# mLSTM cell with a squared-ReLU FFN: rounding of the weights shared between engines, sigmoid gates, the first decay rows through TensorE, and the first FFN group in two halves

## The chip, the cores and the metric

The kernel runs on one core of a Trainium2 chip. The time is device microseconds of one execution, as the median of several runs. One more execution is recorded by the hardware profiler; its times of single instructions are what the text argues from. The engines are TensorE (PE; its weight loads are listed as PEld), VectorE (DVE), ScalarE (ACT), GpSimd (POOL) and SyncE (SP), whose queue issues most transfers.

## The reference

```python
# q, k, v, o_gate: (4, 8, 768, 40); i_gate, f_gate: (4, 8, 768); float32
for t in range(S):
    m_new = np.maximum(f_gate[:, :, t] + m, i_gate[:, :, t])
    f_stab = np.exp(f_gate[:, :, t] + m - m_new)
    i_stab = np.exp(i_gate[:, :, t] - m_new)
    m = m_new
    C = f_stab[:, :, None, None] * C + i_stab[:, :, None, None] * np.einsum('bhd,bhe->bhde', vt, kt)
    n = f_stab[:, :, None] * n + i_stab[:, :, None] * kt
    h_tilde = np.einsum('bhde,bhe->bhd', C, qt)
    nq = np.einsum('bhd,bhd->bh', n, qt)[:, :, None]
    o = 1.0 / (1.0 + np.exp(-o_gate[:, :, t]))
    y[:, :, t] = o * h_tilde / np.maximum(np.abs(nq), 1.0)
...
x = y.transpose(0, 2, 1, 3).reshape(3072, 320)
h = np.maximum(x @ w_in, 0.0)          # w_in: (320, 2048), float64
return (h * h @ w_out).astype(np.float32)   # w_out: (2048, 320), float64
```

## The kernel before, in words

The recurrence runs in 24 chunks of 128 tokens (six for each of the four sequences); the FFN takes four chunks at a time as a group of 512 tokens, six groups in all. Everything is float32. The order of the work on every engine is the order in which the program is written: each engine works through its own list, and SyncE issues its transfers in program order, so that one that must wait holds back those behind it.

At the start `do_gates` (L206) turns the gates into A, the sum of the logarithms of the decays in a chunk, with two scans on VectorE; A goes to DRAM (L215) and comes back as `A_bc`, one row for all partitions (`load_A`, L243). A chunk then has five steps:

- `weigh` (L251): GpSimd adds A_bc and the input's exponent (L255), cuts off the future (L259), ScalarE takes exp (L265): W. Then the output gate 1/(1+exp(-o)): VectorE, ScalarE, VectorE, VectorE (L268 to L271). GpSimd scales the values (L274).
- `transposes` (L278): TensorE turns k and q, ScalarE copies kT and VectorE qT (L287).
- `scores` (L289): sixteen short matmuls, two heads of a pair side by side (L296), then VectorE multiplies by W to P (L301).
- `attend` (L305): the state's share (hi, L312), the state's update (dC, L319), the chunk's own share (hp, L326), then VectorE and GpSimd put them together (L332 to L358); x is the row that the FFN takes.
- `turn_rows` (L360): TensorE turns x, ScalarE copies it into xT (L368).

The weights come as float64, as pairs of 32-bit words. `Rounding` brings them in pieces of 128 rows by 512 (w_in, ten pieces) or by 320 columns (w_out, sixteen), three ahead, and rounds each to float32: six VectorE instructions (L172 to L188) build the truncated value and the remainder, GpSimd adds the two (L191), VectorE puts the sign on (L158), one step later. The first group's four chunks are worked off alone, with two rounding steps beside each; then w_out's pieces are rounded beside the eight parts of the first group's first FFN matmul.

That matmul is `ffn1` (L372): a part makes two slices of d_ff for 512 tokens, four matmuls of 128 rows (L382) and two of 64 rows side by side (L387), then ScalarE's relu (L390) and VectorE's square (L391). The second is `ffn2` (L393, L398): two halves for each chunk. From the ninth part of group 0 on, each chunk of the recurrence is spread over four parts of the FFN.

Of the kernel before, what the change touches and what calls it, by code (L numbers as in the profile page):

```python
# [9 lines left out]
F32 = mybir.dt.float32  # L10
# [6 lines left out]
P = 128  # L17
# [6 lines left out]
# exp of anything below -104 is 0 in float32  # L24
# [4 lines left out]
def kernel(  # L29
# [36 lines left out]
    GT = 4                   # chunks in an FFN group  # L66
    NG = NT // GT
    W = GT * P
    KR = DM - 2 * P          # rows of the last slice of d_model
# [3 lines left out]
    ld = ctx.enter_context(tc.tile_pool(name="ld", bufs=4))  # L73
    prep = ctx.enter_context(tc.tile_pool(name="prep", bufs=3))
# [6 lines left out]
    first = ExitStack()      # what only the start needs; the FFN's tiles lie there later  # L81
    gates = first.enter_context(tc.tile_pool(name="gates", bufs=1))
    conv_in = first.enter_context(tc.tile_pool(name="conv_in", bufs=2))
# [9 lines left out]
    keep = gates.tile([BH, NB, P], F32)  # L93

# [4 lines left out]
    def make_consts():  # L99
# [7 lines left out]
        # 1 where the row's head of the pair is the column's  # L107
# [9 lines left out]
    in_pieces = []  # L117
    for f0 in range(0, DFF, 512):
        for a in range(2):
            in_pieces.append((w_in[:, a, f0 : f0 + 512], [(slice(0, P), win_w[a * P : (a + 1) * P, f0 : f0 + 512, :])]))  # L120
# [383 lines left out]
```

## Time and profile before

| | us |
|---|---|
| median of 3 runs | 705.58 |
| lowest and highest | 704.78, 705.85 |
| span of the profiled execution | 704.2 |
| TensorE busy in it | 600.5 |
| VectorE busy | 343.4 |
| GpSimd busy | 152.6 |
| ScalarE busy | 123.2 |

The execution's time has been given with its span alone; the median of the runs lies 1.4 us above this span. Busy times are sums over the whole span and mix stages, so windows and the chain of waits have to say which engine bounds which stage. A row of the timeline has the start, the duration, engine, line, operation, what is written and read, and in brackets how long the engine had been idle and who ended that. A row of the groups has the busy time, the mean in nanoseconds of one instruction, and the idle time ahead of them. A mean contains what instructions were held up while they ran.

### The profile page before, as it was taken

The page shows a single profiled execution, that of the slowest core. Times are in us where ns is not written, and L with a number is a line of the kernel's source. Part 1 is how long each engine was busy: PE and PEld are TensorE (multiplying, and loading weights), DVE is VectorE, ACT ScalarE, POOL GpSimd, SP SyncE. Part 2 cuts the span into 40 slices and gives each one's busy share as a digit, 9 for nine tenths or more (in the row PEclk, how much of TensorE's full clock was granted, in tenths as well). Part 3 has the DMA queues.
Part 4 walks back from the last instruction along what each step waited for, and adds up shares of the span by engine and source line. Part 5 has one row for each costly group of instructions (what it writes and reads, how often), then busy time and mean ns, then how long its engine had stood idle before and what let it go on. Part 6 is the DMA issues. An engine that isn't in the chain of part 4 may idle for free.

```text
span 704.2 us, 7122 instructions
## 1 busy us (share of the span) xinstructions
PE 600.5 (85%) x2708; PEld 384.3 (55%) x2708; DVE 343.4 (49%) x621; ACT 123.2 (17%) x242; POOL 152.6 (22%) x159
## 2 busy tenths in 40 slices
PE   1236566919469999999999999999999999999998
PEld 1136554414147754477644777554776457763475
DVE  6588895978873335542344523354334434302200
ACT  1201100111011113210231211133111321102200
POOL 1444432322322320321122123202230222000000
PEclk9999856968769999999999999999999999999999
DMA  9976673432514331332132224221330000000000
GB/s 158 233 156 123 123 111 81 76 86 76 107 35 86 76 47 31 67 69 56 48 68 39 56 60 78 47 56 43 76 76 22 0 1 1 19 20 0 1 19 19
DMA packets 141297, 44.79 MB, mean 64 GB/s; under 512 B 109424, under 2 KB 138096, under 8 KB 141264
## 3 DMA queue, kind: packets, MB, share of 16 engines
q1 hardware_dynamic: 141264, 44.35, 31.5%
q8 instruction: 21, 0.34, 0.2%
q14 instruction: 12, 0.10, 0.1%
HBM read 40.30 MB, written 4.03 MB: 63 GB/s over the span
## 4 chain that ended last, share of the span: by engine, by line
PE 68%; DVE 21%; POOL 3%; issue 2%; ACT 2%; SPq 2%; DMA 1%; POOLq 0%; ACTq 0%; DVEq 0%
PE o_ps L398 30%; PE h_ps L382 18%; PE h_ps L387 5%; PE hp L326 4%; DVE og L271 4%; PE sc L296 4%; DVE g L391 3%; PE hi L312 2%; DVE mag L172 2%; PE dC L319 2%; DVE top L182 2%; DVE rem L188 2%; PE tp L283 2%; SPq L241 1%; DVE mag L173 1%
## 5 line engine op out<-in xcount | busy, mean ns | idle before, releaser
L398 PE MATMUL o_ps<-w_out,g 128*128 128x320 f32 x768 | 216.0, 438 | 0.0
L382 PE MATMUL h_ps<-xT,w_in 128*128 128x512 f32 x384 | 179.6, 611 | 0.0
L398 PEld LDWEIGHTS o_ps<-w_out,g 128*128 128x128 f32 x768 | 144.8, 192 | 58.9 <-issue 2.6
L391 DVE TENSOR_TENSOR g<-r_sb 128x512 f32<-128x512 f32 x96 | 63.6, 704 | 135.0 <-ACT r_sb L390 135.0
L382 PEld LDWEIGHTS h_ps<-xT,w_in 128*128 128x128 f32 x384 | 70.5, 193 | 85.3 <-issue 80.1
L296 PE MATMUL sc<-qT,kT 40*128 40x128 f32 x384 | 35.9, 329 | 70.8 <-DVE qT L287 44.6
L390 ACT ACTIVATE r_sb<-h_ps 128x512 f32<-128x512 f32 x96 | 52.2, 595 | 211.9 <-PE h_ps L387 211.9
L296 PEld LDWEIGHTS sc<-qT,kT 40*128 40x128 f32 x384 | 30.6, 227 | 84.0 <-issue 57.2
L191 POOL TENSOR_TENSOR rem<-rem,top 128x320 f32<-128x320 f32 (+1 forms) x26 | 32.1, 1236 | 110.8 <-DVE rem L188 110.8
L387 PE MATMUL h_ps<-xT,w_in 64*128 64x512 f32 x192 | 54.2, 641 | 0.0
L301 DVE TENSOR_TENSOR P_sb<-sc,W_sb 128x512 f32<-128x512 f32 x48 | 30.8, 684 | 45.3 <-PE sc L296 45.3
L326 PE MATMUL hp<-va,P_sb 128*128 128x41 f32 x384 | 51.7, 299 | 0.7 <-ACT xT L368 0.7
L271 DVE RECIPROCAL og<-og 128x320 f32<-128x320 f32 x24 | 51.7, 2153 | 0.8
L326 PEld LDWEIGHTS hp<-va,P_sb 128*128 128x128 f32 x384 | 50.5, 212 | 0.9 <-ACT xT L368 0.9
L255 POOL TENSOR_TENSOR W_sb<-A_bc,b_T 128x1024 f32<-128x1024 f32 x24 | 45.7, 1905 | 14.7 <-DMA A_bc<-a_rows 14.5
L345 POOL TENSOR_TENSOR C_sb<-C_sb,Cd 128x328 f32<-128x328 f32 x16 | 14.1, 884 | 152.7 <-DVE C_sb L337 152.4
L270 DVE TENSOR_SCALAR og<-og 128x320 f32<-128x320 f32 x24 | 12.4, 518 | 69.1 <-ACT og L269 69.1
L404 ACT COPY y_sb<-o_ps 128x320 f32<-128x320 f32 x24 | 10.2, 426 | 204.7 <-PE o_ps L398 204.7
L265 ACT ACTIVATE W_sb<-W_sb 128x1024 f32<-128x1024 f32 x24 | 25.4, 1057 | 60.0 <-POOL W_sb L259 60.0
L358 POOL COPY x_sb<-x_sb 128x64 f32<-128x64 f32 x24 | 6.9, 289 | 126.6 <-DVE x_sb L357 126.6
L387 PEld LDWEIGHTS h_ps<-xT,w_in 64*128 64x128 f32 x192 | 14.4, 184 | 36.4 <-issue 36.4
L319 PE MATMUL dC<-vw,kq 128*128 128x82 f32 x160 | 23.8, 297 | 10.1 <-DVE P_sb L301 10.1
(63 smaller groups left out, 445.9 us busy)
## 6 DMA issues: line engine op xcount, KB each, us to landing
A_bc<-a_rows SPq DMA_DIRECT2D x24, 512.0 KB, 4.4
raw<-in_moe_w_out_dram SPq DMA_DIRECT2D x16, 320.0 KB, 2.9
kq<-in_k_dram SPq DMA_DIRECT2D x26, 160.0 KB, 3.3
kq<-in_q_dram SPq DMA_DIRECT2D x26, 160.0 KB, 4.3
va<-in_v_dram SPq DMA_DIRECT2D x26, 160.0 KB, 3.8
o_sb<-in_o_gate_dram SPq DMA_DIRECT2D x26, 160.0 KB, 3.8
raw<-in_moe_w_in_dram SPq DMA_DIRECT2D x8, 512.0 KB, 4.1
out_dram<-y_sb SPq DMA_DIRECT2D x24, 160.0 KB, 1.8
```

Source lines behind the costliest of these rows:

```text
L191: nc.gpsimd.tensor_tensor(rem[:], rem[:], top[:].bitcast(F32), op=ALU.add)
L255: nc.gpsimd.tensor_tensor(d["W"][:], d["A"][:], b_T[:, b, c, :].unsqueeze(2).to_broadcast([P, H, P]), op=ALU.add,)
L271: nc.vector.reciprocal(d["og"][:], d["og"][:])
L296: nc.tensor.matmul(sc[i][:, j, :], lhsT=d["kT"][rows, j, :], rhs=d["qT"][rows, j, :], start=True, stop=True,)
L301: nc.vector.tensor_tensor(d["P"][:, i], sc[i][:], d["W"][:].rearrange("p (j two) t -> p j two t", two=2)[:, :, i, :], op=ALU.mult,)
L319: nc.tensor.matmul(dC[:, j].rearrange("p h d -> p (h d)"), lhsT=d["kq"][:, 0, 2 * j : 2 * j + 2, :].rearrange("p h d -> p (h d)"), rhs=d[" ...
L326: nc.tensor.matmul(hp[:, h, :], lhsT=d["P"][:, h % 2, h // 2, :], rhs=d["va"][:, h, :], start=True, stop=True,)
L382: nc.tensor.matmul(h[:], lhsT=w_in[:, a, fb * P : (fb + 1) * P], rhs=xT[:, a, :], start=(a == 0), stop=False,)
L387: nc.tensor.matmul(hs[i][:], lhsT=w_in2[rows, p, :], rhs=xT[rows, 2, :], start=False, stop=True)
L390: nc.scalar.activation(r[:], hs[i][:], AF.Relu)
L391: nc.vector.tensor_tensor(st["g2"][:, 2 * p + i, :], r[:], r[:], op=ALU.mult)
L398: nc.tensor.matmul(o_ps[:], lhsT=st["g2"][:, fb, j * P : (j + 1) * P], rhs=w_out[:, fb, :], start=(fb == 0), stop=(fb == NF - 1),)
```

## The change

- The rounding is spread out: ScalarE takes the absolute value of the high word, read as a float, and turns the low word into a float just above 2, whose last bits carry the rounding (two ACTIVATEs); VectorE bounds the high word, shifts it by three bits, and puts the sign in with an exclusive or; GpSimd adds the two words as 32-bit integers, which gives the rounded weight. The buffers of raw words are four, those of the two intermediate tiles two each; w_in and w_out are one list of pieces, ordered as the first FFN matmul takes them.
- The output gate is one ACTIVATE with Sigmoid, in place, for runs of 2, 2, 4, 8 and 8 chunks; the gates have loads of their own.
- For chunks 0 and 1 A does not come through DRAM: TensorE spreads it over the partitions with a matmul against a selector (`weigh_near`), in two halves of four heads.
- The gates' input i and the store of A are issued by ScalarE; one subtraction of the gate stage is GpSimd's; the buffers of A_bc and of W are two where they were three.
- The first group's first FFN matmul runs in two halves of 256 tokens (`ffn1_half`), each of four quarters with four slices of d_ff; the first half starts when two chunks are through, with the rounding of w_in beside it and that of w_out beside the second half.

The core of the diff:

```diff
+        nc.gpsimd.memset(sel[:], 0.0)
+        nc.gpsimd.affine_select(
+            sel[:], sel[:], compare_op=ALU.not_equal, fill=1.0, base=0, pattern=[[-1, H], [0, P]], channel_multiplier=1,
+        )
...
+        def words(self):
...
+            nc.scalar.activation(mag[:, :w], raw[:, :, 1].bitcast(F32), AF.Abs)
+            low = conv.tile([P, 512], F32, name="low")
+            nc.scalar.activation(low[:, :w], raw[:, :, 0].bitcast(U32), AF.Copy, bias=2.0, scale=2.0 ** -51)
+            self.a.append((mag, low))
+
+        def join(self):
...
+            nc.vector.tensor_scalar(
+                mag, mag, scalar1=word_as_float(0x38000000), scalar2=word_as_float(0x47EFFFFF),
+                op0=ALU.max, op1=ALU.min,
+            )
+            nc.vector.tensor_scalar(bits, bits, scalar1=3, scalar2=None, op0=ALU.logical_shift_left)
+            nc.vector.scalar_tensor_tensor(
+                bits, in0=self.raws[n][:, :w, 1], scalar=-0x80000000, in1=bits,
+                op0=ALU.bitwise_and, op1=ALU.bitwise_xor,
+            )
+            nc.gpsimd.tensor_tensor(dst.bitcast(I32), bits, low.bitcast(I32), op=ALU.add)
+            self.b.append(None)
+            self.fetch()
...
         def step(self):
...
+            if len(self.b) < len(pieces):
+                if len(self.a) == len(self.b):
+                    self.words()
+                self.words()
+                self.join()
...
     def do_gates():
         nc.vector.tensor_tensor_scan(m_sb[:], f_sb[:], i_sb[:], -1e30, op0=ALU.add, op1=ALU.max)
+        nc.gpsimd.tensor_tensor(i_sb[:], i_sb[:], m_sb[:], op=ALU.subtract)
...
-        nc.sync.dma_start(A_d[:, :], A_sb[:])
-        nc.vector.tensor_tensor(i_sb[:], i_sb[:], m_sb[:], op=ALU.subtract)
+        nc.scalar.dma_start(A_d[:, :], A_sb[:])
...
+    def sigmoid(s):
+        nc.scalar.activation(st[s]["og"], st[s]["og"], AF.Sigmoid)
...
+    def weigh_near(s):
...
+        for i in range(2):
+            hh = slice(i * H2, (i + 1) * H2)
+            A = ps_h.tile([P, H2, P], F32, name="A_ps", tag="h_ps")
+            for h in range(H2):
+                nc.tensor.matmul(
+                    A[:, h, :], lhsT=sel[:, i * H2 + h, :],
+                    rhs=A_sb[:, c * P : (c + 1) * P], start=True, stop=True,
+                )
+            Wh = d["W"][:, hh, :]
+            nc.vector.tensor_tensor(Wh, A[:], b_T[:, b, c, hh].unsqueeze(2).to_broadcast([P, H2, P]), op=ALU.add)
+            nc.scalar.activation(d["dec"][:, hh], A[:, :, P - 1], AF.Exp)
+            nc.gpsimd.affine_select(
+                Wh, Wh, compare_op=ALU.is_ge, fill=-1e30, base=0, pattern=[[0, H2], [1, P]], channel_multiplier=-1,
+            )
+            nc.scalar.activation(Wh, Wh, AF.Exp)
...
-        d["og"] = prep.tile([P, H, D], F32, name="og")
-        nc.vector.tensor_scalar_max(d["og"][:], d["o"][:], -88.0)
-        nc.scalar.activation(d["og"][:], d["og"][:], AF.Exp, scale=-1.0)
-        nc.vector.tensor_scalar_add(d["og"][:], d["og"][:], 1.0)
-        nc.vector.reciprocal(d["og"][:], d["og"][:])
...
+    def ffn1_half(g, half, pp):
...
+        for i in range(2):
+            for n in range(2):
+                fb = 4 * pp + 2 * n + i
+                for a in range(2):
+                    nc.tensor.matmul(
+                        hs[i][:, n, :], lhsT=w_in[:, a, fb * P : (fb + 1) * P], rhs=xT[:, a, cols],
+                        start=(n == 0 and a == 0), stop=False,
+                    )
...
+    for half in range(2):
+        for u in range(4):
+            s = 2 * (half + 1) + u // 2
+            if u % 2 == 0:
+                score(s)
+                turn_rows(s - 1)
+            else:
+                if u == 1:
+                    for r in range(s, s + 2 + 2 * half):
+                        sigmoid(r)
+                attend_on(s)
+            for _ in range(IN_DONE[u] - rounding.done if half == 0 else 4):
+                rounding.step()
+            ffn1_half(0, half, u)
+            if u % 2 == 0:
+                weigh_on(s + 1)
+            else:
+                transposes(s + 1)
+            if half == 0:
+                load_o(4 + u)
+    assert rounding.done == len(pieces)
+    turn_rows(5)
...
-    for n in range(NU * NG):
+    for n in range(NPAIR, NU * NG):
```

`IN_DONE` is (3, 5, 8, 10): so many pieces are rounded before quarters 0 to 3 of the first half. Where things stand on the engines is shown at three places. On VectorE, beside the first group's first FFN matmul, the order of before has this for one piece of w_out (`raw` are the words, `rem` the remainder, `g` the squared rows):

```order
L172 TENSOR_SCALAR mag<-raw 128x320
L173 TENSOR_SCALAR mag<-mag 128x320
L179 TENSOR_SCALAR top<-mag 128x320
L182 SCALAR_TENSOR_TENSOR top<-mag,top 128x320
L186 TENSOR_SCALAR mag<-top 128x320
L188 SCALAR_TENSOR_TENSOR rem<-raw,mag 128x320
L158 SCALAR_TENSOR_TENSOR w_out<-raw,rem 128x320
L391 TENSOR_TENSOR g_723<-r_sb 128x512 x2
```

Two such pieces stand in a part, and the squares of a part behind them. In the changed kernel the last piece of a quarter of the second half, and what follows it, reads:

```order
L183 TENSOR_SCALAR mag<-mag 128x320
L187 TENSOR_SCALAR mag<-mag 128x320
L188 SCALAR_TENSOR_TENSOR mag<-raw,mag 128x320
L475 TENSOR_TENSOR g_448<-r_sb 128x2x256 x2
L335 COPY qT<-tp 128x512
L354 TENSOR_TENSOR P_sb<-sc,W_sb 128x512 x2
```

Three instructions a piece are left, four pieces stand in a quarter, and the squares, the copy of qT and P stand behind all four. On GpSimd, at the same place, the order of before (`Cd` and `C_sb` are the state, `W_sb` the weighing of a chunk to come):

```order
L191 TENSOR_TENSOR rem<-rem,top 128x320 x2
L340 TENSOR_TENSOR Cd<-C_sb,dec 128x328
L345 TENSOR_TENSOR C_sb<-C_sb,Cd 128x328
L358 COPY x_sb<-x_sb 128x64
L191 TENSOR_TENSOR rem<-rem,top 128x320 x4
L255 TENSOR_TENSOR W_sb<-A_bc,b_T 128x1024
L259 AFFINE_SELECT W_sb<-W_sb 128x1024
```

and of the changed kernel:

```order
L192 TENSOR_TENSOR w_out<-mag,low 128x320 x4
L304 TENSOR_TENSOR W_sb<-A_bc,b_T 128x1024
L308 AFFINE_SELECT W_sb<-W_sb 128x1024
L393 TENSOR_TENSOR Cd<-C_sb,dec 128x328
L398 TENSOR_TENSOR C_sb<-C_sb,Cd 128x328
L411 COPY x_sb<-x_sb 128x64
L192 TENSOR_TENSOR w_out<-mag,low 128x320 x8
```

The add now writes the weight itself, and each add stands directly behind one VectorE instruction of its piece and ahead of the weighing and the state. On TensorE, before, the first FFN matmul of group 0 stands behind all four chunks of the group (`tp` are transposes, `sc` scores, `h_ps` the first FFN matmul):

```order
L367 MATMUL tp<-ident,x_sb 128x128 x3
L296 MATMUL sc<-qT,kT 128x128 x8
L382 MATMUL h_ps<-xT,w_in 128x512 x4
L387 MATMUL h_ps<-xT,w_in_99 128x512 x2
L312 MATMUL hi<-C_sb,qT 128x82 x4
```

and in the changed kernel behind the second chunk's rows:

```order
L420 MATMUL tp<-ident,x_sb 128x128 x3
L331 MATMUL tp<-ident,kq_89 128x128 x8
L344 MATMUL sc<-qT,kT 128x128 x8
L420 MATMUL tp<-ident,x_sb 128x128 x3
L459 MATMUL h_ps<-xT,w_in 128x256 x8
L466 MATMUL h_ps<-xT,w_in_100 128x256 x4
L365 MATMUL hi<-C_sb,qT 128x82 x4
```

The half matmuls have 256 columns instead of 512, twice as many of them, and chunk 2's attend comes behind the first quarter.

More of the change, by code (lines that the diff above doesn't have):

```diff
@@ L446 @@
-    assert rounding.n == len(in_pieces) and not rounding.last
+    for _ in range(3):
+        rounding.fetch()
+    load(1)
+    load_o(0)
+    load_o(1)
+    rounding.fetch()
+    transposes(0)
+    do_gates()
+    rounding.words()
+    weigh_near(0)
+    values(0)
+    transposes(1)
+    scores(0)
+    rounding.step()
+    weigh_near(1)
+    values(1)
     first.close()
     ffn = ctx.enter_context(tc.tile_pool(name="ffn", bufs=2))
-    conv_out = ctx.enter_context(tc.tile_pool(name="conv_out", bufs=2))
@@ L458 @@
         if at == 0:
-            do(scores, s)
+            do(score, s)
         if at == 1:
```

211 lines of the change are left out of this document (120 added, 91 removed).

## The prediction

> **What bounds the kernel now.** I read the page first, then a table of time windows, then the chain of waits around the place where the first FFN group hands over to its second matmul, and then the list of who waited for whom in the first 200 us. The page gives the span, and two rows of 40 slices of 17.6 us each: the busy tenths of VectorE (DVE) and the TensorE clock that was granted, in tenths.
>
> ```profile
> span 704.2 us, 7122 instructions
> DVE  6588895978873335542344523354334434302200
> PEclk9999856968769999999999999999999999999999
> ```
>
> VectorE is at 5 to 9 tenths for the first eleven slices (about 195 us) and at half of that or less afterwards; the clock dips only there. Two windows say the same of TensorE (PE, then weight loads, VectorE, ScalarE, GpSimd, clock):
>
> ```profile
> 180.00:200.00 20.00, 3.12 (x9) 0.87 (x7) 15.05 (x27) 3.25 (x6) 7.41 (x7) 0.66 0.31 92
> 300.00:400.00 100.00, 99.60 (x472) 63.33 (x471) 40.92 (x73) 20.24 (x40) 18.29 (x19) 1.00 0.27 55
> ```
>
> From 300 to 400 us TensorE is busy 99.6 of 100 us: nothing but its own work bounds that stage. From 180 to 200 us it is busy 3.1 of 20 us, and VectorE 15. The chain and the waits name the border between the two stages and who is late ahead of it:
>
> ```profile
> 200.31 2.08 PE sc L296 x16
> 202.39 6.74 PE o_ps L398 x16
> ...
> POOL rem L191 <- DVE rem L188: 101.9, 24, 12.9
> PE sc L296 <- DVE qT L287: 26.0, 2, 16.2
> ```
>
> At 200.31 us the scores of chunk 6 start, then the second FFN matmul of group 0. Ahead of that GpSimd waits 102 us for VectorE's rounding, and TensorE waits for VectorE's copies. So the kernel is a start of 200.3 us bound by VectorE and a tail of 704.2 - 200.3 = 503.9 us bound by TensorE. The changed kernel enters its last loop at the same place (chunk 6's scores, then group 0's second matmul) and runs the same TensorE work from there. I keep the tail at 503.9 us and work out only when chunk 6's scores start. The 1.4 us between this span and the median of 705.58 us are added at the end. Runs spread over 1.1 us, so 0.2% (1.4 us) is what can be told from no change.
>
> **The change, part by part.** *Rounding.* Seven VectorE instructions per piece become three (a max/min, a shift, a combination), two go to ScalarE, and GpSimd's add now makes the result. The nearest rows are those of the same form, 512 and 320 wide:
>
> ```profile
> L173 DVE TENSOR_SCALAR mag<-mag 128x512 f32<-128x512 f32 x10 | 5.2, 521 | 0.3
> L179 DVE TENSOR_SCALAR top<-mag 128x512 int32<-128x512 int32 x10 | 4.3, 427 | 0.3
> L182 DVE SCALAR_TENSOR_TENSOR top<-mag,top 128x512 int32<-128x512 int32 x10 | 6.9, 692 | 0.3
> L173 DVE TENSOR_SCALAR mag<-mag 128x320 f32<-128x320 f32 x16 | 5.8, 361 | 0.6
> L179 DVE TENSOR_SCALAR top<-mag 128x320 int32<-128x320 int32 x16 | 5.2, 327 | 0.5
> L182 DVE SCALAR_TENSOR_TENSOR top<-mag,top 128x320 int32<-128x320 int32 x16 | 7.9, 492 | 0.6
> ```
>
> On VectorE alone a piece costs 0.52 + 0.43 + 0.69 = 1.64 us (512) or 0.36 + 0.33 + 0.49 = 1.18 us (320). But the add of a piece runs beside the VectorE work of the next, and the timeline shows what that does:
>
> ```profile
> 34.40 1.38 POOL L191 TENSOR_TENSOR rem<-rem,top 128x512 f32<-128x512 f32 x1 [7.68 <-DVE rem L188]
> 34.69 1.37 DVE L173 TENSOR_SCALAR mag<-mag 128x512 f32<-128x512 f32 x1
> ...
> 125.76 0.32 DVE L172 TENSOR_SCALAR mag<-raw 128x320 int32<-128x320 int32 x1
> 125.92 0.87 POOL L191 TENSOR_TENSOR rem<-rem,top 128x320 f32<-128x320 f32 x1 [12.94 <-DVE rem L188]
> 126.11 0.87 DVE L173 TENSOR_SCALAR mag<-mag 128x320 f32<-128x320 f32 x1
> ...
> 139.56 1.04 POOL L191 TENSOR_TENSOR rem<-rem,top 128x320 f32<-128x320 f32 x1 [2.40 <-DVE rem L188]
> 139.80 1.35 DVE L391 TENSOR_TENSOR g<-r_sb 128x512 f32<-128x512 f32 x1
> ```
>
> One scalar instruction slips in ahead of the add (125.76); the next (126.11) takes 0.87 us for 0.33 and ends 0.19 us behind the add. So in the change a piece's max/min slips in, its shift waits for the add of the piece before: 0.08 us to the add, 0.87, 0.19, then 0.49 for the combination make 1.63 us per 320 piece. For 512, from the pair at 34.4: 0.08 + 1.38 + 0.28 + 0.69 = 2.45 us. The integer add itself stands in no row; I take the float add's 0.87 and 1.38, which moves the same bytes, with half (only a gain of some 6 us, since VectorE's own work then shows) and twice as bounds.
>
> The last pair shows that the square (two operands out of SBUF) is held as well, 1.35 us for 0.70. The Trainium skill differs here: Advanced Engine Details and Errata, VectorE Performance Modes, names only two-port instructions as blocked by GpSimd. By that the squares and the gate products behind an add would run through, and the sum would be some 3 us less; the row at 139.80 speaks against it.
>
> ScalarE's two reads of a piece run one piece ahead, beside VectorE; at the relu's 0.60 us per 512 (below) twice that is under the 2.45 us per piece, and at double price it would come level.
>
> *Weighing, gates and the first rows.* The first two chunks' decay rows come over TensorE instead of a round trip through DRAM; the gates' reciprocal leaves VectorE (a gain in the tail that TensorE's 99.6% hides). The rows that I use:
>
> ```profile
> 10.48 0.94 DVE L217 TENSOR_TENSOR i_sb<-i_sb,A_sb 32x768 f32<-32x768 f32 x1
> 12.20 0.82 PE L221 MATMUL tp<-ident,A_sb 32*128 32x32 f32 x6
> 41.55 3.55 PE L326 MATMUL hp<-va,P_sb 128*128 128x41 f32 x16
> 115.45 5.01 PE L382 MATMUL h_ps<-xT,w_in 128*128 128x512 f32 x8
> 121.45 1.12 PE L312 MATMUL hi<-C_sb,qT 128*128 128x82 f32 x8
> 125.04 3.68 PE L382 MATMUL h_ps<-xT,w_in 128*128 128x512 f32 x8
> 128.65 1.13 PE L387 MATMUL h_ps<-xT,w_in 64*128 64x512 f32 x4
> ...
> 129.08 0.49 DVE L332 TENSOR_TENSOR num<-hi,eA_T 128x328 f32<-128x328 f32 x1
> 131.94 0.49 DVE L357 TENSOR_TENSOR x_sb<-x_sb,dm 128x320 f32<-128x320 f32 x1
> ...
> L391 DVE TENSOR_TENSOR g<-r_sb 128x512 f32<-128x512 f32 x96 | 63.6, 704 | 135.0 <-ACT r_sb L390 135.0
> L390 ACT ACTIVATE r_sb<-h_ps 128x512 f32<-128x512 f32 x96 | 52.2, 595 | 211.9 <-PE h_ps L387 211.9
> L255 POOL TENSOR_TENSOR W_sb<-A_bc,b_T 128x1024 f32<-128x1024 f32 x24 | 45.7, 1905 | 14.7 <-DMA A_bc<-a_rows 14.5
> L301 DVE TENSOR_TENSOR P_sb<-sc,W_sb 128x512 f32<-128x512 f32 x48 | 30.8, 684 | 45.3 <-PE sc L296 45.3
> L259 POOL TENSOR_SCALAR_AFFINE_SELECT W_sb<-W_sb 128x1024 f32<-128x1024 f32 x24 | 26.2, 1092 | 1.8
> L265 ACT ACTIVATE W_sb<-W_sb 128x1024 f32<-128x1024 f32 x24 | 25.4, 1057 | 60.0 <-POOL W_sb L259 60.0
> L287 DVE COPY qT<-tp 128x512 f32<-128x512 f32 x24 | 15.9, 662 | 5.8 <-PE tp L283 5.8
> L227 ACT ACT_TABLE_LOAD x1 | 1.3, 1283 | 0.7 <-PEq L488 0.7
> ```
>
> *Stage A, to the second chunk's output.* Gate work ends at 11.42 us now; one subtraction moves to GpSimd: 10.5. Twelve small transposes (11.42 to 13.02): 12.1. TensorE then runs cold: eight decay matmuls twice (unseen; four pairs of scores take 2.08, so 0.52 each one by one, 4.2, bounds 2.1 and 4.2), transposes, two scores and the state product at 2.1 each as for scores, and 3.55 for the output: 12.1 + 8.4 + 8.4 + 3.55 = 32.4, and 1.3 of waits for a copy (0.6) and a first product (0.7): 33.7. VectorE: the rest of the output about 2.0, a piece 1.64, P 2 x 0.68: 38.7. The second output on TensorE 3.55, its VectorE tail 2.5 (129.08 to 132.43 is 3.35 for all, 0.8 of it early): 44.8.
>
> *Stage B, to the first half of FFN matmuls.* Chunk 2's weights on GpSimd (behind the second output's copy in its queue) and ScalarE 1.9 + 1.1 + 1.06, a piece on ScalarE 1.2, a copy 0.6, scores 2.1, three transposes and a copy 1.4: 9.3. The first half starts at 54.1 us.
>
> *Stage C, first half.* A half part has as many columns as a part now: 125.04 to 128.65 and 1.13 make 4.7, and 1.33 more when it starts cold (5.01 against 3.68): four times 6.0 is 24.1. Two chunks' attends: TensorE 3.6 (121.45 to 125.04) and VectorE's tail 2.55, 12.3 in all. Three times the FFN waits for a pair of pieces: 1.64 + 2.45 + 1.46 = 5.55, 16.7 in all. Two turns to the next scores: two relus 1.2, a square 0.7, a copy 0.66, scores 2.1: 9.3. One P: 1.4. Sum 63.7, so 117.8 us.
>
> *Stage D, second half.* Here VectorE is the bound. Per quarter four pieces, 1.18 + 3 x 1.63 = 6.1, and two squares of which the second waits for the last add, 1.5: 7.6. A chunk has two quarters, P 1.4, a copy 0.66, an attend 3.35, 1.0 for instructions held by the weighing (1.9 and 1.1 on GpSimd right behind the adds), and 2.1 for scores: 23.7. Two chunks less one scores: 45.3. Chunk 6's scores start at 163.1 us against 200.3.
>
> *Tables.* Exp and sigmoid now alternate: six more table loads ahead of that point, at 1.28 each. One could lie on the path, ahead of chunk 2's product with its gate: relu's end, exp 1.06 and 0.2, load 1.28 and a sigmoid of about 0.5 take 3.1 us, while TensorE's 3.6 and VectorE's first steps run beside them: hidden. The Trainium skill, ScalarE: Activation LUTs, What ACT_TABLE_LOAD costs, puts a switch at 2.66 us with its drain. By that, an estimate from that page, the gate would come level or some 0.8 us late, and the sum be that much more; this trace has one load and cannot show a drain.
>
> *Sum.* 163.1 + 503.9 = 667.0 us of span, with 1.4 around it: 668 us.
>
> **The rivals.** *Faster: TensorE warm and VectorE less held.* If adds held VectorE only as far as its own work (1.28 and 1.74 us per piece with gaps), 16 x 0.35 + 1.8 + 2.0 go, four warm starts save 5.3, and a warm stage A about 5: some 20 us, 649 us. For it: after 8 us of dense work the clock was full (121.45). Against: the start stays broken by waits. 0.20.
>
> *A queue.* SyncE's list is in program order, and a load that must wait for TensorE stands ahead of later pieces and decay rows.
>
> ```profile
> SPq L241 <- PE dC L319: 18.6, 2, 15.4
> ```
>
> One load blocked it for 15.4 us now. In the change chunk 4's loads (released by chunk 0's output, 33.7) stand ahead of pieces, chunk 3 and its decay rows, which are due at about 50. If these come 12 us late: 680 us. 0.15.
>
> *Slower: the integer add.* It makes every weight and stands between VectorE's steps. Each 0.87 us more per 320 piece (1.38 per 512) costs 16 x 0.87 + 6 x 1.38 = 22 us. The gain of 37 us is gone when the add takes 2.7 times the float add; at three times it is 712 us. For it: no integer work on GpSimd stands in this trace. Against: same bytes, same shape. 0.06.
>
> *No effect*, since VectorE stays the bound of the start: its work per piece would have to stay at 3.3 us, and three instructions can't make that. 0.02.
>
> **How the numbers follow.** The forecast has 0.57. The range runs from the warm rival (648) to an add at twice its price (690) and a little of a late queue on top, 694. Faster by over 0.2%: forecast, warm and queue, 0.57 + 0.20 + 0.15, and a share of the no-effect case: 0.93. Same 0.01, slower 0.06.
>
> **What would show it.** Chunk 6's scores start near 163 us and the first half of FFN matmuls near 54. The shift (L187) has a mean far above 0.33 at 320, the add (L192) one of 0.9 to 1.0. TensorE's wait ahead of L459 is for L192, and in the second half for VectorE's copy of qT. The tail from chunk 6's scores is 504 us. Wrong would be: TensorE dense from 60 us on, a long wait of GpSimd for decay rows, or an add of 2 us and more.

## The result, and the profile after

The changed kernel takes 674.64 us (median of 4 runs, 673.16 to 675.48) against 705.72 us (4 runs, 704.78 to 707.17): a ratio of 0.9558 with a 95% interval of 0.9542 to 0.9575. The profiled execution took 673.16 us with a span of 671.4 us, so 1.8 us lie around the span.

The page of the changed kernel, with the same rows as before; a slice is 16.8 us now:

```profile
span 671.4 us, 7338 instructions
DVE  7362455779412333321333123332113432202200
PEclk9999666779799999999999999999999999999999
```

The start has shrunk from eleven slices to ten, and the clock dips as before. (The clock row is no full measure of TensorE's pace: it has 1.00 from 53.8 to 57 us, where sixteen scores take 2.08 us that take 1.16 us at 85.03.) The chain that ended last, up to the border between start and tail (start, duration, engine, tile, line, count):

```profile
53.81 2.08 PE sc L344 x16
85.03 1.18 PE sc L344 x16
120.66 1.18 PE sc L344 x16
146.81 2.10 PE sc L344 x16
172.22 2.08 PE sc L344 x16
174.30 1.90 PE o_ps L482 x3
```

Chunk 6's scores, after which only TensorE's own work counts, start at 172.22 us where they started at 200.31. The tail is 671.4 - 172.2 = 499.2 us where it was 503.9. So 28.1 us of the gain lie in the start and 4.7 in the tail.

The groups of the rounding (busy, mean ns of one, idle time ahead), and the waits of TensorE and VectorE between the scores of chunk 2 and those of chunk 6 (total, times, longest):

```profile
L187 DVE TENSOR_SCALAR mag<-mag 128x320 int32<-128x320 int32 x16 | 12.2, 765 | 0.5
L192 POOL TENSOR_TENSOR w_out<-mag,low 128x320 int32<-128x320 int32 x16 | 14.1, 880 | 30.8 <-DVE mag L188 30.8
L192 POOL TENSOR_TENSOR w_in<-mag,low 128x512 int32<-128x512 int32 x10 | 12.9, 1294 | 23.8 <-DVE mag L188 23.8
...
L267 ACT ACT_TABLE_LOAD x5 | 6.4, 1283 | 0.1
```

```profile
DVE g L475 <- ACT r_sb L474: 34.2, 7, 9.4
PE h_ps L459 <- POOL w_in L192: 19.1, 6, 6.3
PE sc L344 <- DVE qT L335: 10.2, 3, 6.8
```

The integer add takes about what single float adds took (0.88 and 1.29 us for 0.87 and 1.38), and the shift behind it takes 0.77 us where an unheld one takes 0.33. TensorE waits for weights that have just been rounded, six times, and VectorE for TensorE and the relu: in this stage the two take turns. The experiments ask which of these things the gain and the loss hang on.

### The profile page after: what moved, and what is told of

The parts are those of the page before. It is cut to its first block, busy times and chain, and to the rows that moved or that the text cites. A ratio compares the mean times of both kernels' runs of the same rounds, so it can differ in the third digit from the quotient of the medians.

```text
span 671.4 us, 7338 instructions
## 1 busy us (share of the span) xinstructions
PE 609.7 (91%) x2836; PEld 406.4 (61%) x2836; DVE 233.0 (35%) x447; ACT 162.2 (24%) x309; POOL 149.0 (22%) x162
## 4 chain that ended last, share of the span: by engine, by line
PE 83%; DVE 10%; POOL 2%; issue 2%; ACT 1%; DMA 0%; POOLq 0%; DVEq 0%; ACTq 0%
PE o_ps L482 31%; PE h_ps L435 21%; PE h_ps L440 6%; PE hp L379 6%; PE sc L344 4%; PE h_ps L459 3%; PE dC L372 3%; PE tp L331 2%; DVE mag L187 2%; PE hi L365 2%; DVE mag L188 1%; DVE g L475 1%; PE tp L420 1%; PE A_ps L288 1%; DVE mag L183 1%
## 5 line engine op out<-in xcount | busy, mean ns | idle before, releaser
L435 PE MATMUL h_ps<-xT,w_in 128*128 128x512 f32 x320 | 146.9, 602 | 0.0
L444 DVE TENSOR_TENSOR g<-r_sb 128x512 f32<-128x512 f32 x80 | 52.0, 691 | 152.8 <-ACT r_sb L443 152.8
L435 PEld LDWEIGHTS h_ps<-xT,w_in 128*128 128x128 f32 x320 | 57.7, 190 | 69.9 <-issue 65.2
L443 ACT ACTIVATE r_sb<-h_ps 128x512 f32<-128x512 f32 x80 | 43.5, 595 | 172.9 <-PE h_ps L440 172.9
L459 PE MATMUL h_ps<-xT,w_in 128*128 128x256 f32 x128 | 44.6, 517 | 20.2 <-POOL w_in L192 19.1
L459 PEld LDWEIGHTS h_ps<-xT,w_in 128*128 128x128 f32 x128 | 33.0, 267 | 30.1 <-POOL w_in L192 21.7
L440 PE MATMUL h_ps<-xT,w_in 64*128 64x512 f32 x160 | 45.2, 641 | 0.0
L304 POOL TENSOR_TENSOR W_sb<-A_bc,b_T 128x1024 f32<-128x1024 f32 x22 | 42.4, 1929 | 0.0
L335 DVE COPY qT<-tp 128x512 f32<-128x512 f32 x23 | 15.8, 687 | 73.0 <-PE tp L331 73.0
L331 PE MATMUL tp<-ident,kq 128*128 128x128 f32 x192 | 28.0, 293 | 5.1 <-DMA kq<-in_k_dram 5.1
L322 POOL TENSOR_TENSOR vw<-va,W_sb 128x328 f32<-128x328 f32 x20 | 15.2, 758 | 70.4 <-ACT W_sb L314 68.9
```

What stands on the lines that cost most here:

```text
L304: nc.gpsimd.tensor_tensor(d["W"][:], d["A"][:], b_T[:, b, c, :].unsqueeze(2).to_broadcast([P, H, P]), op=ALU.add,)
L331: nc.tensor.transpose(tp[:, j, :], d["kq"][:, i, 2 * j : 2 * j + 2, :].rearrange("p h d -> p (h d)"), ident[:],)
L435: nc.tensor.matmul(h[:], lhsT=w_in[:, a, fb * P : (fb + 1) * P], rhs=xT[:, a, :], start=(a == 0), stop=False,)
L440: nc.tensor.matmul(hs[i][:], lhsT=w_in2[rows, p, :], rhs=xT[rows, 2, :], start=False, stop=True)
L443: nc.scalar.activation(r[:], hs[i][:], AF.Relu)
L444: nc.vector.tensor_tensor(st["g2"][:, 2 * p + i, :], r[:], r[:], op=ALU.mult)
```

## The experiments

The theory is that of the prediction: the start is bound by VectorE, the gain comes from its smaller work (rounding first, gate second), and what is left is VectorE held by GpSimd. The rivals: the new order (halves, rows over TensorE) brings the gain; or TensorE's order bounds the start and the hold is hidden. Each kernel is the changed one with the edit shown, unless said otherwise, and was timed against the kernel before. The expectations speak of "the second half" and "the first half" of the first group's first FFN matmul.

| kernel | us (runs) | ratio to before, 95% |
|---|---|---|
| changed | 674.64 (673.16-675.48) | 0.9558 (0.9542-0.9575) |
| without the add | 663.63 (662.54-666.68) | 0.9410 (0.9385-0.9435) |
| add twice | 693.46 (691.28-695.02) | 0.9823 (0.9798-0.9849) |
| old rounding | 721.02 (719.87-722.20) | 1.0216 (1.0200-1.0232) |
| old gate | 696.57 (696.17-697.63) | 0.9874 (0.9858-0.9891) |
| before, with the new rounding alone | 670.28 (669.52-670.64) | 0.9506 (0.9492-0.9520) |
| rows through DRAM | 674.68 (674.25-675.04) | 0.9570 (0.9555-0.9584) |
| eight pieces later | 661.62 (661.14-662.40) | 0.9382 (0.9367-0.9398) |
| without halves | 657.46 (656.67-658.28) | 0.9326 (0.9312-0.9340) |
| squares on ScalarE | 673.07 (672.45-673.44) | 0.9537 (0.9522-0.9552) |
| subtraction on VectorE | 674.44 (674.01-675.34) | 0.9559 (0.9543-0.9575) |
| without halves, weighing early | 655.27 (652.57-655.74) | 0.9276 (0.9249-0.9302) |
| the same, pieces spread | 650.15 (649.40-650.82) | 0.9213 (0.9197-0.9229) |

**The hold, taken away and doubled.**

```diff
-                mag, mag, scalar1=word_as_float(0x38000000), scalar2=word_as_float(0x47EFFFFF),
+                mag, mag, scalar1=word_as_float(0x38000000), scalar2=word_as_float(0x38000000),
...
-                bits, in0=self.raws[n][:, :w, 1], scalar=-0x80000000, in1=bits,
+                dst.bitcast(I32), in0=self.raws[n][:, :w, 1], scalar=-0x80000000, in1=bits,
...
-            nc.gpsimd.tensor_tensor(dst.bitcast(I32), bits, low.bitcast(I32), op=ALU.add)
```

> The changed kernel without GpSimd's integer add: VectorE's combination writes the weight, the low words are computed and not used, and all weights are held to plus or minus 2. Theory (VectorE is held by the add of the piece before, 1.71 us per 320-wide piece and 2.46 per 512-wide one): a piece falls to what the first, unheld piece of a quarter shows, 1.12 us from its max/min to the next one; 16 x 0.59 is 9.4 us, of which TensorE's cold half parts take some back, and the waits of the FFN halves for the last add of a quarter (about 1.3 us, four times) go: 662 us, 656 to 668. The shift's mean falls from 0.77 to 0.33 us. Rival (TensorE's order bounds the start, the hold is hidden): 673 to 675 us.

```diff
             nc.gpsimd.tensor_tensor(dst.bitcast(I32), bits, low.bitcast(I32), op=ALU.add)
+            nc.gpsimd.tensor_tensor(dst.bitcast(I32), bits, low.bitcast(I32), op=ALU.add)
```

> The changed kernel with GpSimd's integer add made twice per piece, the second over the same words with the same result. Theory: each doubling costs 16 x 0.87 + 6 x 1.38 = 22 us as the prediction's third rival has it, so 696 us, 688 to 700. If the held instruction slips through the gap between the two adds, VectorE is held less and GpSimd's own 1.75 us per piece set the pace: not less than 675 + 16 x 0.1, about 680. Rival (hold hidden): 673 to 677 us.

VectorE and GpSimd in the timelines, without the add and with two (start, duration, engine, line):

```profile
122.74 0.32 DVE L183 TENSOR_SCALAR mag<-mag 128x320 f32<-128x320 f32 x1
123.09 0.33 DVE L187 TENSOR_SCALAR mag<-mag 128x320 int32<-128x320 int32 x1
123.45 0.49 DVE L188 SCALAR_TENSOR_TENSOR w_out<-raw,mag 128x320 int32<-128x320 int32 x1
123.86 0.32 DVE L183 TENSOR_SCALAR mag<-mag 128x320 f32<-128x320 f32 x1
```

```profile
131.34 0.86 POOL L192 TENSOR_TENSOR w_out<-mag,low 128x320 int32<-128x320 int32 x1 [12.84 <-DVE mag L188]
131.47 0.92 DVE L187 TENSOR_SCALAR mag<-mag 128x320 int32<-128x320 int32 x1
132.28 0.86 POOL L193 TENSOR_TENSOR w_out<-mag,low 128x320 int32<-128x320 int32 x1
132.42 1.07 DVE L188 SCALAR_TENSOR_TENSOR mag<-raw,mag 128x320 int32<-128x320 int32 x1
133.63 0.86 POOL L192 TENSOR_TENSOR w_out<-mag,low 128x320 int32<-128x320 int32 x1 [0.49 <-DVE mag L188]
```

Without the add a piece comes every 1.12 us; with two, the first holds the shift (0.92) and the second the combination (1.07 for 0.49), and the next piece's first add comes 2.29 us later. The times move by -11.0 and +18.8 us. Both agree with the theory; "the hold is hidden" falls twice. (The first also spares the FFN quarters the wait for a quarter's last add, which the expectation put at some 1.3 us four times; its 11.0 us are not the hold alone.) The second shows the limit of the sum: a piece grew by some 0.6 to 0.9 us, not by the whole second add, since one instruction slips in between the two.

**Rounding and gate, one at a time.** In the next two kernels the old rounding (`magnitude` as in the kernel before, the sign one step later, one buffer of `mag` instead of two) and the old gate (in the chunk's weighing) stand in the new order.

```diff
+            done, self.last = self.last, None
+            if self.n < len(pieces):
+                self.last = self.magnitude(self.n)
+                self.n += 1
+            self.finish(done)
...
-            nc.scalar.activation(mag[:, :w], raw[:, :, 1].bitcast(F32), AF.Abs)
...
-            nc.scalar.activation(low[:, :w], raw[:, :, 0].bitcast(U32), AF.Copy, bias=2.0, scale=2.0 ** -51)
...
+            if half == 0 or u == 3:
+                rounding.flush()
```

> The changed kernel with the old rounding: seven VectorE instructions and a float add per piece, nothing on ScalarE; the order, the sigmoid, the first rows and the halves stay. Theory (the gain is the smaller VectorE work): a 320-wide piece costs 3.3 us instead of 1.71 and a 512-wide one 4.9 instead of 2.46; 16 x 1.6 in the second half and 7 x 2.4 in the first, some 42 us: 717 us, 705 to 728, no better than the kernel before. Rival (the gain is the order, above all the halves, which give TensorE work from 57 us on): at most 685 us.

```diff
-        nc.scalar.activation(st[s]["og"], st[s]["og"], AF.Sigmoid)
...
+        nc.vector.tensor_scalar_max(og, og, -88.0)
+        nc.scalar.activation(og, og, AF.Exp, scale=-1.0)
+        nc.vector.tensor_scalar_add(og, og, 1.0)
+        nc.vector.reciprocal(og, og)
```

> The changed kernel with the old output gate: bound, exp, plus one and reciprocal, three VectorE instructions of 0.46, 0.52 and 2.15 us per chunk, placed in each chunk's weighing as before. Theory: VectorE bounds the start, so eight gates of 3.13 us, 25 us, come nearly whole to the path in the second half (three gates, 9.4 us) and in part in the first stages, while the tail hides them under TensorE: 690 us, 684 to 700. Rival (TensorE's order bounds): 674 to 678 us.

The new order with the old rounding is slower than the kernel before: the rounding is worth 46.4 us here, the gate 21.9. The rival that the order makes the gain falls. The gate's share has a second place. These are TensorE's scores of a few chunks in the tail, in the changed kernel, in the one with the old gate and in the kernel before:

```profile
196.66 1.16 PE L344 MATMUL sc<-qT,kT 40*128 40x128 f32 x16
...
551.30 1.06 PE L344 MATMUL sc<-qT,kT 40*128 40x128 f32 x16
```

```profile
216.10 1.16 PE L349 MATMUL sc<-qT,kT 40*128 40x128 f32 x16
...
574.29 1.16 PE L349 MATMUL sc<-qT,kT 40*128 40x128 f32 x16 [0.20 <-DVE qT L340]
```

```profile
225.94 1.16 PE L296 MATMUL sc<-qT,kT 40*128 40x128 f32 x16
...
584.13 1.16 PE L296 MATMUL sc<-qT,kT 40*128 40x128 f32 x16 [0.20 <-DVE qT L287]
```

From chunk 7's to chunk 22's scores it is 354.64 us in the first and 358.19 us in both others: wherever the reciprocal stands on VectorE, its copy of qT comes 0.2 us late in seven of these chunks by the profile's marks. With the restart behind it such a wait costs some 0.47 us; an eighth chunk falls back by 0.26 us without a mark. The expectation had the tail hide the gates.

**The rounding alone, and the rows.** The first kernel is the one before with the new rounding and nothing else; the diff is against the kernel before. The second is the changed one with `load_A` for chunks 0 and 1; `weigh_far` is `weigh_near` with A_bc in place of A_ps.

```diff
-                self.last = self.magnitude(self.n)
...
+            self.words()
+            dst = self.pieces[n][0]
+            mag, low = self.a[n]
+            bits = mag[:].bitcast(I32)
...
+            nc.gpsimd.tensor_tensor(dst.bitcast(I32), bits, low[:].bitcast(I32), op=ALU.add)
```

> The kernel before with the new rounding alone: old order (four chunks, then eight whole parts of the first FFN matmul), old gate, rows through DRAM. Theory (the start is bound by VectorE, whatever the order): 16 x (3.3 - 1.71) + 10 x (4.9 - 2.46), some 49 us less on VectorE, of which TensorE's own work in the start takes a few back: 663 us, 656 to 674. Rival (the new order is needed, so that the smaller work on VectorE becomes time): 685 us or more.

```diff
+    load_A(0)
+    load_A(1)
...
-    weigh_near(0)
+    weigh_far(0)
```

> The changed kernel with the decay rows of chunks 0 and 1 brought through DRAM again; TensorE's 16 cold matmuls of 3.76 us per chunk go, and a store and a load of some 2 and 4.2 us come ahead of chunk 0's weights. Theory (the rows matter little, since stage A is a chain of cold TensorE work either way): 674.6 us, 671 to 679. Rival (the rows over TensorE are a good part of the gain): 682 us or more.

The new rounding alone gives 704.93 - 670.28 = 34.65 us, more than the whole change (the intervals do not meet). So the rest of the change, taken together, costs time, although the gate in it gains. The rows are not the cause: the kernel with rows through DRAM takes the same time. There the first product for W waits until 20.89 us for its rows, and TensorE is rid of 7.5 us of cold matmuls.

**Without the halves.** Chunks 2 and 3 with the last seven pieces of w_in, then `ffn1` whole:

```diff
-    for half in range(2):
-        for u in range(4):
-            s = 2 * (half + 1) + u // 2
...
-            for _ in range(IN_DONE[u] - rounding.done if half == 0 else 4):
...
-            ffn1_half(0, half, u)
...
+    for u in range(4):
+        s = 2 + u // 2
...
+        for _ in range(2 if u < 3 else 1):
...
-    for n in range(NPAIR, NU * NG):
+    for n in range(NU * NG):
...
             ffn1(g, u)
+            if g == 0:
+                for _ in range(2):
+                    rounding.step()
```

> The changed kernel without the halves: chunks 2 and 3 and the last seven pieces of w_in alone, then the first FFN matmul of group 0 in eight whole parts, each with two pieces of w_out behind it, beside chunks 4 and 5, as in the kernel before. Theory (VectorE's work bounds the start, so the halves themselves bring nothing, and their waits between pieces and half parts may cost): chunks 2 and 3 end at about 88 us, eight parts of 1.44 + 3.42 us and two chunks of 5.4 us, with 3 us of holds, end at about 143: 645 us, 640 to 665. Rival (the halves make the gain, since TensorE has FFN work from 57 us on): 685 us or more.

This is the loss: 17.2 us less than with the halves, though not the 645 us of the theory. Two stretches of the start (busy us and count of PE, weight loads, VectorE, ScalarE, GpSimd; then the granted clock) with TensorE's scores of chunk 3, first in the changed kernel and then in this one, where the last line is the scores of chunk 5:

```profile
53.80:91.40 37.60, 24.97 (x128) 19.07 (x128) 16.35 (x30) 11.14 (x20) 9.94 (x10) 0.82 0.41 90
91.40:120.60 29.20, 18.86 (x87) 14.34 (x86) 13.40 (x23) 8.66 (x15) 10.83 (x10) 0.71 0.45 97
85.03 1.16 PE L344 MATMUL sc<-qT,kT 40*128 40x128 f32 x16 [1.68 <-DVE qT L335]
```

```profile
53.80:91.40 37.60, 24.34 (x123) 21.75 (x123) 24.60 (x43) 15.58 (x26) 20.15 (x20) 1.00 0.63 144
91.40:120.60 29.20, 26.58 (x108) 13.92 (x107) 17.44 (x35) 12.94 (x26) 9.98 (x12) 1.00 0.58 118
74.78 2.08 PE L344 MATMUL sc<-qT,kT 40*128 40x128 f32 x16 [9.40 <-ACT kT L335]
123.26 2.08 PE L344 MATMUL sc<-qT,kT 40*128 40x128 f32 x16 [5.27 <-ACT kT L335]
```

At 120.66 us the changed kernel has half of the FFN matmul done and comes to the scores of chunk 4. At 123.26 us this one has the same half done too (four whole parts), and comes to the scores of chunk 5, with eight pieces of w_out rounded besides. With the halves, a quarter of FFN matmuls stands in TensorE's queue ahead of the chunk's attend and waits for pieces that VectorE and GpSimd are just making; VectorE then waits for that quarter's relu and for the attend behind it. VectorE is busy 16.35 of 37.6 us there, 24.60 without halves. The clock column, 1.00 for 0.82 and 0.71, misleads here: this kernel's scores of chunk 3 take 2.08 us and the changed kernel's 1.16, so that in the first stretch it is this kernel whose TensorE is cold. In the second stretch it is faster: its whole parts of eight matmuls take 4.76, 3.68, 3.70 and 3.60 us, where the last fourteen matmuls of the changed kernel's two quarters take 5.76 and 4.70. What it has gained by then is VectorE's work done meanwhile, eight pieces of 1.71 us. How the 17.2 us divide between the turns and TensorE's pace was not measured.

**Which steps of the second half were late.** Two small edits, for the two places where the profile shows VectorE held by something other than the add, timed together:

```diff
             nc.scalar.activation(r2, hs[i][:], AF.Relu)
-            nc.vector.tensor_tensor(g4[:, :, i, :], r2, r2, op=ALU.mult)
+            if half == 1 and pp % 2 == 0:
+                nc.scalar.activation(g4[:, :, i, :], r2, AF.Square)
+            else:
+                nc.vector.tensor_tensor(g4[:, :, i, :], r2, r2, op=ALU.mult)
```

> The changed kernel with the squares of the second half's first and third quarter on ScalarE instead of VectorE; nothing else. In the changed kernel these squares run beside GpSimd's weighing and take 2.95 and 3.13 us a pair where an unheld pair takes 1.29. Theory (the weighing holds them on the path, part of the 5 us that the second half came late): 1 us each, behind which the attend still waits for TensorE, so 672.6 us, 671.5 to 673.5. Rival (the hold is covered by TensorE's part of the attend): 674 to 675 us.

```diff
-        nc.gpsimd.tensor_tensor(i_sb[:], i_sb[:], m_sb[:], op=ALU.subtract)
...
+        nc.vector.tensor_tensor(i_sb[:], i_sb[:], m_sb[:], op=ALU.subtract)
         nc.vector.tensor_tensor(i_sb[:], i_sb[:], A_sb[:], op=ALU.subtract)
```

> The changed kernel with the subtraction of the gate stage (i minus m) back on VectorE, behind the second scan. Theory (GpSimd's 2.56 us of it hold VectorE's subtraction of the same time, 2.44 us for 0.94): A is ready at 10.1 us instead of 11.6, the rows for b_T at 12.0 instead of 12.6, and the first half of FFN matmuls starts 0.6 to 1.5 us earlier, at 55.8 to 56.7: 673.5 us. Rival (the start of the chain is covered by cold TensorE work or by loads): first half at 57.3 us, 674.6 us.

The squares' hold is worth about 1.4 us (674.44 - 673.07): the runs of the two kernels, on one chip, are 672.45 to 673.44 and 674.01 to 675.34. Against the changed kernel, timed on another occasion, the intervals overlap, so this is just what can be told. The profile shows 1.6 us at one of the two places (from chunk 5's to chunk 6's scores 23.84 us for 25.41) and nothing at the other (from chunk 4's to chunk 5's 26.78 us for 26.15). There, with the squares on ScalarE, VectorE waits for the sigmoid, which stands behind GpSimd's weighing, its exp and a table load:

```profile
135.16 1.28 ACT L267 ACT_TABLE_LOAD   x1
136.95 0.49 DVE L409 TENSOR_TENSOR x_sb<-num,og 128x320 f32<-128x320 f32 x1 [0.75 <-ACT og L267]
```

Later in the same chunk ScalarE waits 1.96 us for a piece's transfer. The subtraction is worth nothing. The first quarter of FFN matmuls starts at 57.24 us with it on VectorE, where it started at 57.29: the matmuls that spread A start at 13.94 us in the one and 13.97 in the other, because a wait of the transposes for the copy of b_T stands in the place of the hold.

**Pieces later.** Two pieces instead of four beside each quarter of the second half, and eight beside the first two units of the tail:

```diff
-            for _ in range(IN_DONE[u] - rounding.done if half == 0 else 4):
+            for _ in range(IN_DONE[u] - rounding.done if half == 0 else 2):
...
-            ffn2(g, *divmod(u - NPAIR, 2))
+            j, part = divmod(u - NPAIR, 2)
+            if g == 0 and j < 2:
...
+                j, part = part, j
+            ffn2(g, j, part)
+            if g == 0 and u < NPAIR + 2:
+                for _ in range(4):
+                    rounding.step()
```

> The changed kernel with eight of w_out's sixteen pieces taken out of the second half (two per quarter in place of four) and rounded beside the first two parts of the second FFN matmul, which for that take the first eight slices of d_ff for chunks 0 and 1 and then the other eight. Theory (VectorE's held pieces set the second half): 8 x 1.71 = 13.7 us less there, of which TensorE's cold half parts and the relu behind them take some 5 back, and the tail hides the eight pieces: 666 us, 662 to 670. Rival (TensorE's order sets the second half): 673 us or more, and the tail may lose 2 to 4 us where VectorE is late: up to 679.

13.0 us less, nearly all of the 13.7, and more than expected. These are the scores of chunk 5 and the FFN matmuls right behind them, in the changed kernel, and the same with the scores of chunk 6 in this one:

```profile
146.81 2.08 PE L344 MATMUL sc<-qT,kT 40*128 40x128 f32 x16 [6.83 <-DVE qT L335]
149.52 5.16 PE L459 MATMUL h_ps<-xT,w_in 128*128 128x256 f32 x16
```

```profile
142.23 1.16 PE L344 MATMUL sc<-qT,kT 40*128 40x128 f32 x16 [2.20 <-DVE qT L335]
143.71 3.62 PE L459 MATMUL h_ps<-xT,w_in 128*128 128x256 f32 x16
160.85 1.16 PE L344 MATMUL sc<-qT,kT 40*128 40x128 f32 x16 [3.72 <-ACT low L174]
```

TensorE has waited 2.20 us for 6.83 and is not cold: the same sixteen matmuls take 3.62 us for 5.16, at a granted clock of 1.00 for 0.70. The expectation had not counted that. The tail from 160.85 us on is 660.6 - 160.85 = 499.75 us: the eight pieces are hidden there.

**A version that beats both.** In the kernel without halves TensorE's longest waits are those for kT. ScalarE's row there, from the timeline (what ended its idle time in brackets):

```profile
149.08 0.48 ACT L174 ACTIVATE low<-raw 128x320 f32<-128x320 uint32 x1
...
153.41 1.06 ACT L314 ACTIVATE W_sb<-W_sb 128x1024 f32<-128x1024 f32 x1 [3.74 <-POOL W_sb L308]
154.37 0.46 ACT L421 COPY xT<-tp 128x384 f32<-128x384 f32 x1
154.73 0.59 ACT L335 COPY kT<-tp 128x512 f32<-128x512 f32 x1
```

The copy stands behind the exp of the next chunk's W, which waits for GpSimd's weighing, which stands behind the adds. The next kernel puts the weighing ahead of the third part; the last one also spreads the pieces (four of w_in beside chunks 2 and 3, two beside each part, three of w_out beside the first unit of the tail with the order of `ffn2` shown above).

```diff
+        if at == 2 and n < NPAIR:
+            do(weigh_on, s + 1)
...
-        if at == 2:
+        if at == 2 and n >= NPAIR:
             do(weigh_on, s + 1)
```

> The kernel without halves, with the weighing of chunks 5 and 6 ahead of the third part's rounding instead of behind it, where GpSimd is idle for 4.8 us; in the kernel without halves TensorE waits 5.3 us ahead of the scores of chunks 5 and 6, because ScalarE's copy of kT stands behind the exp of the weighing, and that behind GpSimd's adds. Theory (order of ScalarE's queue): both waits go but for about 1 us: 649 us, 646 to 652. Rival (VectorE's held pieces are late just behind that): 655 us or more.

> As the kernel with the early weighing, and the pieces spread further: four instead of seven pieces of w_in beside chunks 2 and 3, two pieces of whichever come next behind each of the eight parts, the last three pieces of w_out beside the first part of the second matmul, which takes its first eight slices for chunks 0 and 1 first. Theory (held pieces between the steps of chunks 2 and 3 are on the path): 3 x 2.46 us less there: 643 us, 640 to 647. Rival (chunks 2 and 3 are bound by their own chain of steps and by ScalarE's queue): as the kernel with the early weighing, within 2 us.

The early weighing gains 2.2 us, not 8, and the rival's figure is the one measured. Its reason is only half right: the 5.3 us became two waits, one for the relu ahead of an FFN part and one for kT still:

```profile
149.36 1.98 PE L435 MATMUL h_ps<-xT,w_in 128*128 128x512 f32 x4 [2.68 <-ACT r_sb L443]
154.68 1.57 PE L344 MATMUL sc<-qT,kT 40*128 40x128 f32 x16 [2.28 <-ACT kT L335]
```

Both are ScalarE's, whose queue holds the words of pieces that wait for GpSimd's adds. Spreading the pieces gains 5.1 us more, where the theory had 7.4 and the rival at most 2; the time lies above the range of 640 to 647, which was built on the 649 us that the early weighing missed. At 650.15 us this version is 7.9% below the kernel before and some 3.6% below the changed one (0.9213 / 0.9558). From 88 us to the scores of chunk 6 the profile marks no wait of TensorE but for ScalarE's results (7.1 us for relus, 2.8 us for kT). That ScalarE's order is what still holds it was not tested.

## Why the prediction was right, and where its steps were off

The forecast of 668 us is 6.6 us below the 674.64 measured, and in the main the mechanism, a start bound by VectorE that is held by GpSimd's adds, is the one that the runs show. That it came so near is in part luck: the start ended 9.1 us late (172.2 us for 163.1) and the tail was 4.7 us short. Step by step:

- **Start and tail, VectorE held by GpSimd.** Right. The pace of pieces came out at 1.71 us (320) for 1.63 and at 2.46 (512) for 2.45. Taking the add away and doubling it moves the time by -11.0 and +18.8 us, as the hold and the wait for the last add ask.
- **The integer add at the float add's price.** Right: 0.88 and 1.29 us. The slower rival had its price from this and is out; its 22 us per doubling came out as 18.8.
- **Stages A and B: 54.1 us.** 57.29 measured. The gate stage ended 2.1 us late: the subtraction on GpSimd took 2.56 us and held VectorE's next one, 2.44 us for 0.94. The sum had counted such holds elsewhere and not here. Undone, it brings the start no further forward, because the transposes then wait for the copy of b_T: the hold has a cover, and the sum had neither the one nor the other. The other 1.1 us are 0.5 in the rest of stage A and 0.6 in stage B, where GpSimd's weighing of chunk 2 takes 3.7 us up to the exp for the 3.0 counted, beside a combination on VectorE that is held for 2.27 us.
- **Stage C: 63.7 us.** 64.5 from 57.29 to P at 121.83 us. The waits for pieces are 19.1 us where 16.7 were counted.
- **Stage D: 45.3 us.** 50.4 measured; this is the term that was most mis-sized: chunk 4 took 27.1 us from its P to chunk 5's for 23.7, and chunk 5 took 23.3 us from its P to chunk 6's scores for 21.6. "Here VectorE is the bound" holds in a chunk's second quarter and not in its first: the squares wait for TensorE's cold quarter (6.48 and 1.13 us) and the relu, and by then the weighing has begun on GpSimd and holds them. In the timeline of the changed kernel:

```profile
123.12 6.48 PE L459 MATMUL h_ps<-xT,w_in 128*128 128x256 f32 x16 [0.57 <-ACT xT L421]
129.53 1.13 PE L466 MATMUL h_ps<-xT,w_in 64*128 64x256 f32 x8
130.34 1.90 POOL L304 TENSOR_TENSOR W_sb<-A_bc,b_T 128x1024 f32<-128x1024 f32 x1
131.33 2.95 DVE L475 TENSOR_TENSOR g<-r_sb 128x512 f32<-128x512 f32 x2 [1.95 <-ACT r_sb L474]
```

  The pair of squares takes 2.95 us for 1.29, and 3.13 us in chunk 5. In chunk 5 the experiment gives 1.6 us for it, which is nearly all that this chunk is late. In chunk 4 taking the squares away gained nothing; there the cold quarter, the relu and the sigmoid behind the table load remain, and how the 3.4 us divide among them was not taken apart. The Trainium skill (Advanced Engine Details and Errata, VectorE Performance Modes) names two-port instructions and no others as blocked by GpSimd. The trace shows more: a square, a tensor_tensor with both operands in SBUF, waits too.
- **The tail: 503.9 us.** 499.2 measured. "A gain in the tail that TensorE's 99.6% hides" was wrong: 3.6 us are the reciprocals' waits, shown with the old gate. A TensorE that is 99.6% busy still has 0.4% of waits, and they were VectorE's (two of 0.20 us in those 100 us, at 368.59 and 393.45). The other 1.2 us are a shorter start behind chunk 6's scores; up to chunk 7's scores it is 24.2 to 25.8 us in the kernels that keep this order, and why was not settled.
- **Tables.** Loads of 1.28 us each, ten more than before. After one at 134.83 us the sigmoid starts at 136.12, so there is no drain to be seen, and the 2.66 us of the Trainium skill (ScalarE: Activation LUTs, What ACT_TABLE_LOAD costs) does not appear. "Hidden" was right of chunk 2, for which it was worked out, but the sum looked at no other place: in chunk 4 the load stands between the weighing's exp (133.77) and the gate's product (136.63) on the chain that ended last.
- **The rivals.** TensorE stayed cold in much of the start: of the eight quarters, two ran their sixteen matmuls at full pace (3.70 us, at 134.19 and 158.37). SyncE's queue did not show in the changed kernel's trace: in the first 172 us TensorE waited for a transfer only at the start (5.1 us for k), and VectorE 0.5 us for i. What the warm rival priced at 649 us is what the order without halves comes near to (657.46, and 650.15 with the pieces spread), but not by its mechanism: there too TensorE is cold in the start (scores of 2.08 us at 53.66, 74.78 and 91.35 us) and the adds hold VectorE.

What the prediction did not ask is whether a part of the change loses. Its stage C, four quarters, three pairs of pieces and two attends added up one behind the other, says that nothing overlaps there, and this went into the sum as a cost of the start, not as a sign against the order.

## What to carry to other kernels

When several edits come together, sum each stage also for the order without them: a stage whose terms are added one after the other is one in which engines take turns, and giving the bound engine's consumer work earlier there can cost more than it fills. Work of an engine that binds only one stage is best moved to where that engine is idle, and what it costs is seen by taking it out or doubling it. A waiting instruction on the way of a copy (an exp behind GpSimd's queue, a word behind an add) is as costly as the engine that it waits for.

## What the runs showed of the hardware

- GpSimd's add of two 32-bit integer words takes 0.88 us for 128x320 and 1.29 us for 128x512; single float adds of these sizes took 0.87 and 1.38.
- Between two adds of GpSimd that follow directly, one held VectorE instruction ends and the next is held by the second add (a shift 0.92 us for 0.33, a combination 1.07 for 0.49).
- ScalarE's read of every second word takes 0.49 us for 320 columns and 0.66 us for 512, where a relu of 512 out of PSUM takes 0.59 (changed kernel).
- The same sixteen FFN matmuls took 3.62 us at a granted clock of 1.00 (143.71 us, eight pieces later), 5.16 us at 0.70 (149.52, changed kernel) and 6.48 us at 0.57 (123.12, changed kernel). The length of the last wait alone does not tell which: TensorE had waited 2.20, 6.83 and 1.68 us ahead of the scores in front of them.
- The clock row has 1.00 from 53.8 to 57 us in the changed kernel, and up to 120 us without halves, though sixteen scores take 2.08 us in these stretches and 1.16 us elsewhere.
